# A causal convolution and a maxout layer on one core: the first tokens' chunk goes last, and the opening is put in a new order

## The chip, the cores and the metric

The kernel runs on one core of a Trainium2 chip. The metric is the device time of one execution in microseconds (us). Engines are named as in the profile: PE is TensorE (matmuls; PEld is its weight load), DVE is VectorE, ACT is ScalarE, POOL is GpSimd, and SP is the engine whose queue issues the DMAs here.

## The reference

```python
# x (8, 4160, 192), weight_gen (8, 4160, 8 heads, 7 taps); w1, w2, w3 (192, 768), w_out (768, 192)
w = np.exp(weight_gen - weight_gen.max(-1, keepdims=True))
w = w / (w.sum(-1, keepdims=True) + 1e-9)
x_pad = np.concatenate([zeros of 6 tokens, x], axis=1)
x_unf = x_pad[:, idx, :]             # for each token its own and the six tokens before it
a = np.einsum('bshk,bskhg->bshg', w, x_unf.reshape(B, S, 7, 8, 24)).reshape(B * S, 192)
h = np.maximum(np.maximum(a @ w1, a @ w2), a @ w3)
out = h @ w_out                       # (33280, 192)
```

The dense weights come as float64. The kernel sees each as a pair of 32-bit words.

## The kernel before, in words

The 33280 tokens are 260 for each of the 128 partitions. They are worked in 65 chunks of four tokens a partition (TC = 4, so 512 tokens a chunk, CH), and x and weight_gen are loaded for two chunks at a time (a "super"; the first one holds a single chunk). A super's tile of x, xt, has six tokens of halo ahead of its own. For the first tokens of a partition the halo is the tail of the partition before, or zero: such a super is loaded with a zeroing on DVE (L295, memset of the halo) and with row DMAs (L305) behind the main one (L287). There are two buffers for xt, two for wt (the softmax weights), three for the tap products r, two for the sums acc.

A chunk goes through these steps. Softmax for its super: max (DVE, L326), subtract (POOL, L331), exp (ACT, L335), sum (DVE, L340), 1e-9 added (DVE, L344), reciprocal (L348), and the product with the weights (POOL, L352). Then for each of the four tokens of a partition one product of 7 x 192 elements (POOL, L370, `r<-xt,wt`, "a tap product") and its sum over the seven taps (DVE, L382, `acc<-r`). The sums are turned so that features lie on partitions: by PE transposes (L402) for chunks 0 and 1 (ON_TENSOR = 2), by a DVE transpose and 24 block moves on ACT (L432, into `room`) for all others. The turned tokens are split into a high and a low part in the format that PE multiplies fast (xa_hi, xa_lo for features 0 to 127; xc, xb for the remaining 64).

The maxout layer uses max(a·w1, a·w2, a·w3) = a·w1 + max(0, a·(w2-w1), a·(w3-w1)). PE multiplies with the two differences (wa_hi, wa_lo, wb_hi, wb_lo; L802, `up`), ACT applies relu to the first (m, L859), DVE takes the maximum (L867), and the result is split again (h_hi on ACT, h_lo on DVE or POOL, L878). The output products (`down`, L802 too) multiply h with w_out and add a·(w1·w_out), whose matrices wca and wcb are composed once on PE (L750, 24 passes, behind turned weights, L731/L733) and split (L759, L767). The products of every group run as two halves of the PE's rows, lower and upper, at the same time; a nop on SP stands between the halves (L808), and it is queued with the DMA issues.

At the start the weights are made: each block of float64 words becomes one fp32 value by an Abs on ACT (L573), and on DVE a clamp (L579), a shift (L586) and two combinations (L595, L604). Then come differences (POOL, L631, L661) and splits (L643, L673). Blocks of 128 rows of w1, w2, w3 are called `a` (0 to 2), of the other 64 rows `b` (0 to 2), of w_out `down` or `d`.

The order of instructions on each engine is not written by hand. Each step is a `Task` with an engine, a cost, its predecessors, the buffers it holds, and a due time; `Plan.order()` plays these out with the costs and takes, on each engine, the ready task that is due first and whose buffers are free. PE's own order is fixed by the order in which its tasks are added. What comes out is the program: each engine then runs its list in that order, whatever the real durations.

Of the kernel before, what the change touches and what calls it, by code (L numbers as in the profile page):

```python
# [20 lines left out]
class Hold:  # L21


    def __init__(self, pool):
        self.pool, self.users, self.taken, self.tile = pool, 0, False, None


class Task:
    def __init__(self, engine, cost, emit, deps, due, holds, end):
        self.engine, self.cost, self.emit, self.due = engine, cost, emit, due  # L30
        self.holds, self.after = holds, []
        self.end = cost if end is None else end
        self.missing = 0
        for d in deps:
            d.after.append(self)
            self.missing += 1
        for h in holds:
            h.users += 1


class Plan:
# [4 lines left out]
    LATENCY = 0.12  # L46

    def __init__(self, pools):
        self.free = dict(pools)
        self.waiting = {"L": [], "U": []}  # L50
        self.tasks = []

    def add(self, engine, cost, emit, deps=(), due=0.0, holds=(), end=None):
# [3 lines left out]
        if engine in self.FIXED:  # L57
            self.waiting[engine].append(t)
        return t

    def order(self):
        ready, busy, events, done = {}, {}, [], []
        at = dict.fromkeys(self.FIXED, 0)
        for t in self.tasks:
            ready.setdefault(t.engine, [])
            busy.setdefault(t.engine, 0.0)
            if t.missing == 0 and t.engine not in self.FIXED:
                heapq.heappush(ready[t.engine], (t.due, t.n, t))

        def can(t):  # L70
            need = {}
            for h in t.holds:
                if not h.taken:
                    need[h.pool] = need.get(h.pool, 0) + 1
            return all(self.free[p] >= n for p, n in need.items())

        def start(t, now):
            for h in t.holds:
                if not h.taken:
                    h.taken = True  # L80
                    self.free[h.pool] -= 1
# [3 lines left out]
            heapq.heappush(events, (now + t.cost, 0, t.n, t, "free"))  # L85
            heapq.heappush(events, (now + t.end, 1, t.n, t, "given"))
            heapq.heappush(events, (now + t.end + self.LATENCY, 2, t.n, t, "seen"))

        now = 0.0
        while True:  # L90
            for e in ready:
                if busy[e] > now + 1e-9:
                    continue
                if e in self.FIXED:
                    k = at[e]
                    if k < len(self.waiting[e]):
                        t = self.waiting[e][k]
# [33 lines left out]
def lightconv_maxout_kernel(  # L131
# [29 lines left out]
    ON_TENSOR = 2  # L161
    DOWN_AT = 3
    ON_POOL = (1, 4)

# [15 lines left out]
    halves = (slice(0, DB), slice(DB, P))  # L180

# [9 lines left out]
    w1a = const.tile([P, NJ, P], F32, name="w1a")  # L191
    b32 = const.tile([P, NP, 3, P], F32, name="b32")
# [39 lines left out]
    plan = Plan(counts | {"conv": 3})  # L232
# [14 lines left out]
    def vec(n):  # L247
        return 0.15 + 0.00105 * n

    def act(n):  # L250
        return 0.18 + 0.00084 * n

    def gps(n):
        return 0.1 + 0.0024 * n


    PERIOD = 21.0
    FIRST = 22.0

    def needed(c):  # L260
        return FIRST + PERIOD * c
# [4 lines left out]
    def transfer(cost, emit, deps=(), due=0.0, holds=(), on="SP"):  # L266
        issue = plan.add(on, 0.45, emit, deps, due, holds)
        return plan.add("DMA", cost, lambda: None, [issue], due, holds, end=cost + 2.0)
# [4 lines left out]
    def load_super(s):  # L273
        cs = supers[s]
        a, n = cs[0] * TC, len(cs) * TC
        hx, hw = xts[s], wts[s] = hold("xt"), hold("wt")
        due = needed(cs[0]) - 40

# [10 lines left out]
        w = transfer(0.0005 * n * H * K, weights, (), due, [hw])  # L289
        if a >= PAD:  # L290
            t = [transfer(0.0005 * (n + PAD) * D, tokens, (), due + 0.1, [hx])]
        else:
# [4 lines left out]
            t = [transfer(0.0005 * (n + a) * D, tokens, (), due + 0.1, [hx])]  # L297
            for b in range(B):
                on = "ACT" if s == 0 and b % 2 else "SP"

                def rows(b=b, on=on):
                    to = slice(b * PB + 1, (b + 1) * PB)
                    q = nc.scalar if on == "ACT" else nc.sync
                    pin(
                        q.dma_start(  # L305
                            out=buf(hx)[to, :z], in_=xf[to.start - 1 : to.stop - 1, NT - z :]
                        )
                    )

                t.append(transfer(0.1, rows, [zero], due + 0.2, [hx], on))  # L310
# [5 lines left out]
    def softmax(s):  # L316
        n = len(supers[s]) * TC
        due = needed(supers[s][0]) - 32
# [8 lines left out]
            [loads[s][0]], due, [hr, hw],  # L327
# [4 lines left out]
            [a], due + 1, [hr, hw],  # L332
# [3 lines left out]
            [b], due + 2, [hw],  # L336
# [4 lines left out]
            [c], due + 3, [hd, hw],  # L341
        )
        e = plan.add(
            "DVE", 0.3, lambda: pin(nc.vector.tensor_scalar_add(part(hd), part(hd), 1e-9)),  # L344
            [d], due + 3, [hd],
        )
        f = plan.add(
            "DVE", 0.6, lambda: pin(nc.vector.reciprocal(part(hd), part(hd))), [e], due + 3, [hd]  # L348
# [4 lines left out]
            [f], due + 4, [hd, hw],  # L353
# [5 lines left out]
    def taps(c):  # L359
# [3 lines left out]
        due = needed(c)  # L363
        sums = []
        for t in range(TC):
            hr = hold("r")

            def product(t=t, hr=hr):
                pin(
                    nc.gpsimd.tensor_tensor(  # L370
# [661 lines left out]
```

## Time and profile before

| | us |
|---|---|
| median of 3 runs | 1440.14 (1439.23 to 1443.31) |
| profiled execution, its own time | 1444.6 |
| span in the profile | 1442.8 |
| mean granted clock of TensorE | 0.987 |
| PE busy | 1402.0 (97%) |
| ACT, POOL, DVE busy | 1117.3, 1104.2, 1043.4 |

The span is what the profile sees from the first instruction to the last; the execution's own time is 1.8 us longer. In rows of instructions the first number is the start or the busy time, as the sentence ahead says; "x36" is a count, and what follows the second bar is the idle time ahead of them with what ended it. A chunk takes 20.9 us of PE in the steady part.

### The profile page before, as it was taken

How to read it: one execution, taken by the hardware profiler on the slowest of the kernel's cores; microseconds unless marked ns; L12 is line 12 of the kernel's file. 1: busy time of each engine (PE TensorE's matmuls, PEld its weight loads, DVE VectorE, ACT ScalarE, POOL GpSimd, SP SyncE). 2: the span in 40 equal slices, each digit the busy share in tenths (PEclk: the TensorE clock that was granted, in tenths of full speed). 3: DMA queues.
4: the chain of work that ended last, by engine and by line, in shares of the span. 5: the costliest groups of instructions: out<-in, count | busy, mean ns of one | idle time of the engine just before them, and what ended most of it. 6: DMA issues, size and time to landing. Idle time of an engine off the chain costs nothing.

```text
span 1442.8 us, 37119 instructions
## 1 busy us (share of the span) xinstructions
PE 1402.0 (97%) x14878; PEld 1366.1 (95%) x14878; DVE 1043.4 (72%) x1433; ACT 1117.3 (77%) x2828; POOL 1104.2 (77%) x609
## 2 busy tenths in 40 slices
PE   2889999999999999999999999999999999999999
PEld 1579999999999999999999999999999999999998
DVE  7867777777777787777778777877877677777543
ACT  3547878878877887787788778877888887788773
POOL 6769888778877887887788778778877877787421
PEclk9679999999999999999999999999999999999999
DMA  7102111111111111111011111101111111110000
GB/s 249 46 1 79 57 68 57 68 68 57 68 46 46 57 68 68 68 57 64 28 57 68 68 68 57 68 25 67 57 68 68 57 68 44 48 57 24 23 21 26
DMA packets 23405, 85.08 MB, mean 59 GB/s; under 512 B 2768, under 2 KB 9544, under 8 KB 19136
## 3 DMA queue, kind: packets, MB, share of 16 engines
q1 hardware_dynamic: 23112, 82.44, 15.5%
q8 instruction: 116, 1.90, 0.5%
q14 instruction: 57, 0.47, 0.1%
q10 hardware_dynamic: 120, 0.28, 0.1%
HBM read 57.15 MB, written 25.56 MB: 57 GB/s over the span
## 4 chain that ended last, share of the span: by engine, by line
PE 95%; POOL 1%; DMA 1%; ACT 1%; SPq 1%; DVE 1%; issue 0%; POOLq 0%
PE bank L802 95%; POOL r L370 1%; DMA xt<-in_x_dram 1%; SPq L532 1%; DVE den L344 0%; ACT room L432 0%; DMA raw<-in_moe_w_dram 0%; SPq L516 0%; PE bank L733 0%; ACT m L859 0%; POOL wa_lo L643 0%; PE bank L731 0%; ACT wb_hi L684 0%; DVE acc L382 0%; ACT bank L573 0%
## 5 line engine op out<-in xcount | busy, mean ns | idle before, releaser
L370 POOL TENSOR_TENSOR r<-xt,wt 128x1344 f32<-128x1344 f32 x260 | 727.1, 2845 | 143.2 <-DVE acc L382 142.9
L802 PE MATMUL bank<-wo,h_hi 64*128 64x384 f32 x3120 | 675.0, 357 | 0.0
L802 PE MATMUL bank<-wo,h_lo 64*128 64x192 f32 x3120 | 603.4, 249 | 0.0
L432 ACT COPY room<-room 32x128 f32<-32x128 f32 x1512 | 448.4, 297 | 79.0 <-DVE room L421 55.9
L802 PEld LDWEIGHTS bank<-wo,h_lo 64*128 64x128 f32 x3120 | 493.0, 188 | 0.0
L802 PEld LDWEIGHTS bank<-wo,h_hi 64*128 64x128 f32 x3120 | 489.2, 186 | 0.0
L802 PE MATMUL bank<-xa_hi,wa_hi 64*128 64x512 f32 x1560 | 479.9, 394 | 6.0 <-ACT wa_hi L637 3.4
L802 PE MATMUL bank<-xa_hi,wa_lo 64*128 64x512 f32 x1560 | 477.9, 390 | 3.4 <-POOL wa_lo L643 3.3
L802 PE MATMUL bank<-xa_lo,wa_hi 64*128 64x512 f32 x1560 | 476.8, 391 | 0.5 <-DVE xa_lo L460 0.5
L382 DVE TENSOR_REDUCE acc<-r 128x192 f32<-128x1344 f32 x260 | 399.8, 1538 | 0.6 <-POOL r L370 0.3
L859 ACT ACTIVATE m<-bank 128x512 f32<-128x512 f32 x390 | 234.5, 601 | 71.4 <-PE bank L802 66.7
L935 DVE TENSOR_TENSOR o<-bank,ob 128x192 f32<-128x192 f32 x260 | 92.4, 356 | 268.7 <-ACT ob L928 268.5
L802 PE MATMUL bank<-xb,wb_hi 64*128 64x512 f32 x780 | 284.5, 390 | 0.3 <-DVE xb L465 0.3
L802 PE MATMUL bank<-xc,wb_hi 64*128 64x512 f32 x780 | 281.1, 390 | 0.2 <-ACT wb_hi L684 0.2
L802 PEld LDWEIGHTS bank<-xa_hi,wa_hi 64*128 64x128 f32 x1560 | 255.3, 186 | 13.5 <-ACT wa_hi L637 4.3
L802 PEld LDWEIGHTS bank<-xa_hi,wa_lo 64*128 64x128 f32 x1560 | 255.3, 186 | 11.2 <-POOL wa_lo L643 5.6
L802 PEld LDWEIGHTS bank<-xa_lo,wa_hi 64*128 64x128 f32 x1560 | 254.9, 187 | 6.4 <-DVE xa_lo L460 1.5
L802 PE MATMUL bank<-xc,wb_lo 64*128 64x512 f32 x780 | 258.0, 389 | 0.0
L867 DVE TENSOR_TENSOR bank<-bank,m 128x512 f32<-128x512 f32 x260 | 179.0, 689 | 42.2 <-PE bank L802 24.3
L878 POOL TENSOR_TENSOR h_lo<-m,h_hi 128x512 fp32r<-128x512 f32 x130 | 171.7, 1321 | 40.0 <-ACT h_hi L871 39.9
L802 PE MATMUL bank<-wca,xa_hi 64*128 64x384 f32 x520 | 183.4, 353 | 0.0
L878 DVE TENSOR_TENSOR h_lo<-bank,h_hi 128x512 fp32r<-128x512 f32 x260 | 172.4, 681 | 11.4 <-ACT h_hi L871 11.2
(79 smaller groups left out, 2012.5 us busy)
## 6 DMA issues: line engine op xcount, KB each, us to landing
xt<-in_x_dram SPq DMA_DIRECT2D x31, 1344.0 KB, 5.8
out_dram<-o SPq DMA_DIRECT2D x64, 384.0 KB, 2.3
wt<-in_weight_gen_dram SPq DMA_DIRECT2D x32, 224.0 KB, 2.6
h_hi<-in_moe_w_dram SPq DMA_DIRECT2D x6, 256.0 KB, 2.9
xt<-in_x_dram SPq DMA_DIRECT2D x1, 1152.0 KB, 5.8
h_lo<-in_moe_w_dram SPq DMA_DIRECT2D x6, 128.0 KB, 4.0
raw<-in_moe_w_dram SPq DMA_DIRECT2D x3, 256.0 KB, 3.6
room<-in_moe_w_out_dram SPq DMA_DIRECT2D x2, 384.0 KB, 6.4
```

Source lines behind the costliest of these rows:

```text
L370: nc.gpsimd.tensor_tensor(buf(hr).rearrange("p (h g) k -> p k h g", g=G), buf(hx)[:, la + t : la + t + K].rearrange("p k (h g) -> p k h g" ...
L382: pin(nc.vector.tensor_reduce(buf(ha)[:, t], buf(hr), axis=AX.X, op=ALU.add))
L432: pin(nc.scalar.copy(to[:, :, p : p + 32], b[p : p + 32, :, f : f + 32]))
L532: nc.sync.dma_start(out=raw_b()[h, jps[0] : jps[-1] + 1, i].rearrange("p j n w -> p j (n w)"), in_=w[P:].rearrange("p (j o n) -> p j o n", ...
L802: ins = nc.tensor.matmul(buf(hb)[:, :n], w()[h], v()[h], start=half == 0 and first, stop=half == 1 and last,)
L859: lambda: pin(nc.scalar.activation(buf(hm), buf(hb), AF.Relu)), [made], due,
L867: lambda: pin(nc.vector.tensor_tensor(buf(keep), buf(hb), buf(hm), op=ALU.max)),
L878: eng.tensor_tensor(buf(hl)[:, j], buf(keep), buf(hh)[:, j].bitcast(F32), op=ALU.subtract)
L935: nc.vector.tensor_tensor(buf(ho)[:, t], buf(hb)[:, :D], buf(hq), op=ALU.add)
```

## The change

Five things are changed.

1. `place` maps the chunk that the program works on to the tokens that it holds: the program's chunks 0, 1, 2 ... 62 are the tokens' chunks 2, 3 ... 64, and its last two are the tokens' chunks 0 and 1. So the super with the halo rows is the last one. Its row DMAs become four with strided partitions (64, 32, 16 and 8 rows).
2. The due times are no longer worked out from a period: `start_by` goes backwards from the tasks that have one. Costs are new (DVE 0.062 + 0.00104 n instead of 0.15 + 0.00105 n, ACT's block moves 0.31 instead of 0.296, a tap product 2.68 instead of 2.75), the latency is 0.1, and at most eight DMAs are counted in flight.
3. The order in which the opening's tasks are added is written out (`OPENING`), with times for its loads (`LOAD_DUE`).
4. Engines in the opening: three of the first eight tap products go to DVE; eight clamps go to POOL (through a tile `m`, since POOL doesn't get the bank); the differences of a block's two matrices are made together where they can be; the difference of the last `b` block goes to PE (`minus`); two splits go to DVE (L762); POOL takes h_lo of three of six blocks in chunks 0 and 1 rather than two. The `b` loads are six DMAs, not twelve.
5. The 1e-9 is added on ACT (L395), in each super.

```diff
+    place = [*range(2, NC), 0, 1]
-        a, n = cs[0] * TC, len(cs) * TC
+        a, n = place[cs[0]] * TC, len(cs) * TC
...
+            step = 2
+            while step <= PB:
+                def rows(step=step):
+                    to = buf(hx)[step // 2 :: step, :z]
+                    of = xf[step // 2 - 1 :: step, NT - z :][: P // step]
+                    pin(nc.sync.dma_start(out=to, in_=of))
...
+    def start_by(self):
+        for t in reversed(self.tasks):
+            latest = [a.by - self.LATENCY - t.end for a in t.after]
+            if t.due is not None:
+                latest.append(t.due)
+            t.by = min(latest, default=1e6)
...
+    ON_POOL_FIRST = (0, 1, 5)
+    TAPS_ON_VECTOR = ((0, 3), (1, 0), (1, 2))
+    CLAMP_ON_POOL = (("a", 1, 0), ("a", 1, 1), ("a", 2, 0), ("a", 2, 1), ("a", 2, 2), ("b", 1), ("d", 0), ("d", 1),)
...
         e = plan.add(
-            "DVE", 0.3, lambda: pin(nc.vector.tensor_scalar_add(part(hd), part(hd), 1e-9)),
+            "ACT", 0.25,
+            lambda: pin(nc.scalar.activation(part(hd), part(hd), AF.Copy, bias=1e-9)),
...
+            eng, cost = ("DVE", vec(D * K)) if (c, t) in TAPS_ON_VECTOR else ("POOL", 2.68)
...
-                got.append(plan.add("ACT", 0.296, move, [turned], due - 11 + q, [hv]))
+                got.append(plan.add("ACT", 0.31, move, [turned], clock[0] - 2 + q, [hv]))
```

The zeroing of the last super's halo still has no predecessor, and holds its xt buffer from then on.

The new line numbers that matter: clamp L659, shift L665, combinations L674 and L683, tap product L428, sum L440, differences L731, split of the weights L762, products L922, maximum L987, h_lo L998, x loads L337 (L339 and L357 for the last super), weight_gen L332.

DVE in the opening, from the point where the first chunk's sums begin. The kernel before:

```order
L326 TENSOR_REDUCE red<-wt 128x64
L382 TENSOR_REDUCE acc<-r 128x192
L579 TENSOR_SCALAR bank<-bank 128x384
L604 SCALAR_TENSOR_TENSOR wx<-h_hi,bank 128x256
L382 TENSOR_REDUCE acc<-r 128x192
L586 TENSOR_SCALAR bank<-bank 128x384
L595 SCALAR_TENSOR_TENSOR bank<-h_hi,bank 128x256
L382 TENSOR_REDUCE acc<-r 128x192
```

And the changed one, at the same point:

```order
L376 TENSOR_REDUCE red<-wt 128x64
L428 TENSOR_TENSOR r<-xt,wt 128x7x192
L440 TENSOR_REDUCE acc<-r 128x192 x2
L659 TENSOR_SCALAR bank<-bank 128x384 x2
L665 TENSOR_SCALAR bank<-bank 128x384 x2
L674 SCALAR_TENSOR_TENSOR bank<-h_lo,bank 128x384 x2
L683 SCALAR_TENSOR_TENSOR b_68<-h_lo,bank 128x384 x2
L440 TENSOR_REDUCE acc<-r 128x192 x2
```

Sixteen rows stand ahead of the first sum before and 26 now; a tap product on DVE is new, and the sums stand two and two.

SP's queue, from its first row, with the tiles' numbers (xt_135 and so on are uses, not addresses). The kernel before:

```order
L280 DMA wt_133<-in_weight_gen_dram 128x224
L287 DMA xt_135<-in_x_dram 128x768
L516 DMA h_hi_138<-in_moe_w1_dram 128x512
L305 DMA xt_135<-in_x_dram 15x1152 x4
L516 DMA h_hi_138<-in_moe_w2_dram 128x512
L516 DMA h_hi_138<-in_moe_w3_dram 128x512
```

The changed one, behind a first block of the same three weight loads:

```order
L598 DMA h_hi_134<-in_moe_w1_dram 128x512
L598 DMA h_hi_134<-in_moe_w2_dram 128x512
L598 DMA h_hi_134<-in_moe_w3_dram 128x512
L332 DMA wt_144<-in_weight_gen_dram 128x224
L337 DMA xt_146<-in_x_dram 128x1920
L332 DMA wt_150<-in_weight_gen_dram 128x448
```

And nine rows further on, from the last super's load:

```order
L339 DMA xt_136<-in_x_dram 128x1536
L357 DMA xt_136<-in_x_dram 64x1152
L357 DMA xt_136<-in_x_dram 32x1152
L357 DMA xt_136<-in_x_dram 16x1152
L357 DMA xt_136<-in_x_dram 8x1152
L337 DMA xt_262<-in_x_dram 128x2688
L332 DMA wt_277<-in_weight_gen_dram 128x448
L337 DMA xt_668<-in_x_dram 128x2688
```

Two blocks of the weights now head the queue. xt_136 is the last super's x: it is loaded in the opening and read by POOL's last tap products, at the program's end. It holds one of the two xt buffers till then.

POOL in the steady part, around the last tap product of one super and the first of the next, with the tiles' numbers. The kernel before:

```order
L370 TENSOR_TENSOR r_8454<-xt_7231,wt_7222 128x7x192
L460 TENSOR_TENSOR xa_lo_8532<-room_8215,xa_hi_8516 128x512
L465 TENSOR_TENSOR xb_8553<-room_8215,xc_8528 64x512
L370 TENSOR_TENSOR r_8620<-xt_7231,wt_7222 128x7x192
L878 TENSOR_TENSOR h_lo_8366<-m_8598,h_hi_8334 128x512
L370 TENSOR_TENSOR r_8687<-xt_7952,wt_7943 128x7x192
```

The changed one, at the same point:

```order
L428 TENSOR_TENSOR r_8639<-xt_7973,wt_7250 128x7x192
L998 TENSOR_TENSOR h_lo_8703<-m_8685,h_hi_8674 128x512
L549 TENSOR_TENSOR xb_8861<-room_8570,xc_8819 64x512
L544 TENSOR_TENSOR xa_lo_8880<-room_8570,xa_hi_8856 128x512
L403 TENSOR_TENSOR wt_7983<-wt_7983,den_8816 128x448
L381 TENSOR_TENSOR wt_8692<-wt_8692,red_8858 128x448
L428 TENSOR_TENSOR r_8931<-xt_8682,wt_7983 128x7x192
```

One step stands between the two products before, five now.

More of the change, by code (lines that the diff above doesn't have):

```diff
@@ L296, in load_super @@
             )
[L297 to L310, printed above, removed]
+            t = [transfer(0.38 * (n + a), tokens, (), due + 0.1, [hx])]
+            step = 2
[4 more added lines that the diff above has]
+                    pin(nc.sync.dma_start(out=to, in_=of))
+                t.append(transfer(0.38 * z / step, rows, [zero], due + 0.2, [hx]))
+                step *= 2
         loads[s] = w, t
@@ new lines, in difference, with rest, differences_a @@
+        return lambda: buf(hb)[:, : n * m].rearrange("p (i n) -> p i n", i=n), d, [hb]
+    def rest(size, to, of, hi, deps, holds, on):
+        eng = nc.gpsimd if on == "POOL" else nc.vector
+        return plan.add(
+            on, gps(size) if on == "POOL" else vec(size),
+            lambda: pin(eng.tensor_tensor(to(), of(), hi(), op=ALU.subtract)), deps, None, holds,
+        )
+    def differences_a(jp, first, last):
+        pair = slice(2 * jp, 2 * jp + 2)
+        hx, got = of_bank["x", jp]
+        on, then = MODE["a", jp]
+        n = last - first
+        v, d, holds = difference(
+            (n, 2 * P), lambda: buf(hx)[:, first:last],
+            lambda: w1a[:, pair].rearrange("p j n -> p (j n)"), [*got[first:last], one_a[jp]],
+            [hx], on,
+        )
+        of = lambda: v().rearrange("p i (j n) -> p i j n", j=2)
+        place_of = lambda w: w[:, pair, first:last].rearrange("p j i n -> p i j n")
+        hi = plan.add(
+            "ACT", act(2 * n * P), lambda: pin(nc.scalar.copy(place_of(wa_hi), of())), [d], None,
+            holds,
+        )
+        lo = rest(
+            2 * n * P, lambda: place_of(wa_lo), of, lambda: place_of(wa_hi).bitcast(F32), [hi],
+            holds, then,
+        )
+        for i in range(first, last):
+            w_hi[jp, i], w_lo[jp, i] = hi, lo
@@ L939, in down @@
         )
-        a = c * TC
+        a = place[c] * TC
         if c == NC - 1:
@@ L951, in down @@
             )
-    made = plan.add("POOL", 1.0, lambda: make_identity(nc, ident), (), -50)
-    for s in range(len(supers)):
-        load_super(s)
-    load_a(0)
-    load_b([0])
-    load_a(1)
-    load_b([1, 2])
-    load_a(2)
-    load_down()
-    for s in range(len(supers)):
-        softmax(s)
-    for jp in range(NP):
-        prepare_a(jp)
-        prepare_b(jp)
-    for q in range(NP):
-        prepare_down(q)
-    def tokens(c):
-        parts(c, *blocks(c, *taps(c), u_last() + [made]))
@@ L992, in lightconv_maxout_kernel, with downs, ups, singles_down @@
-    for c in (NC - 2, NC - 1):
+    made = plan.add("POOL", 1.0, lambda: make_identity(nc, ident), (), -60)
+    made_minus = plan.add(
+        "ACT", 0.25, lambda: pin(nc.scalar.activation(minus, ident, AF.Copy, scale=-1.0)),
+        [made], -40,
+    )
+    def tokens(c):
+        parts(c, *blocks(c, *taps(c)))
+    def downs(c):
         for t in range(TC):
             down(c, t)
+    def ups(c, j):
+        for i in range(NI):
+            up(c, j, i)
+    def singles_down():
+        for q in range(NP):
+            prepare_down(q)
@@ new lines, in lightconv_maxout_kernel @@
+    step = {
+        "load": load_super, "load a": load_a, "load b": load_b, "load down": load_down,
+        "softmax": softmax, "singles": singles, "singles down": singles_down, "taps": opening_taps,
+        "turn x": turn_tokens, "parts": opening_parts,
+        "a": differences_a, "b": differences_b, "up": ups,
+        "turn": turn_weights, "compose": compose, "down": downs,
+    }
+    for what, *which in OPENING:
+        step[what](*which)
+    for c in range(2, NC):
+        s = super_of[c]
+        if s > 1 and supers[s][0] == c:
+            load_super(s)
+            softmax(s)
+        if c >= ON_TENSOR:
+            tokens(c)
+        for j in range(DOWN_AT):
+            ups(c, j)
+        if c < NC - 1:
+            downs(c - 1)
+        for j in range(DOWN_AT, NJ):
+            ups(c, j)
```

399 lines of the change are left out of this document (218 added, 181 removed), and 6 rows, old and new, of the table OPENING.

## The prediction

> **What bounds the kernel now.** I read the page first, for what ends last.
>
> ```profile
> PE 1402.0 (97%) x14878; PEld 1366.1 (95%) x14878; DVE 1043.4 (72%) x1433; ACT 1117.3 (77%) x2828; POOL 1104.2 (77%) x609
> PE 95%; POOL 1%; DMA 1%; ACT 1%; SPq 1%; DVE 1%; issue 0%; POOLq 0%
> ```
>
> PE is 97% busy, and it is 95% of the chain that ended last. The end of that chain says from when on:
>
> ```profile
> 87.88 4.04 DVE den L344
> 91.92 0.26 DVE wcb L767
> 92.22 1347.23 PE bank L802 x12536
> ```
>
> From 92.22 us PE works without a gap for 1347.23 us. So a change can win in three ways only: PE reaches the same point of its work sooner, PE runs at a better clock after it, or PE has less to do. It can lose if another engine's cycle grows past PE's. PE's waits, first those in the first 92.2 us, then those after 92:
>
> ```profile
> PE bank L402 <- DVE acc L382: 21.8, 4, 16.6
> PE bank L802 <- DVE wcb L767: 5.2, 1, 5.2
> ```
>
> In the opening PE waits for the sums of the tap products; its last wait, 5.2 us, ends at 92.2. Stretches of time (columns: window, its length, busy us and counts of PE, PEld, DVE, ACT, POOL, PE clock, DMA share, GB/s):
>
> ```profile
> 0.00:92.22 92.22, 54.81 (x223) 39.11 (x223) 69.03 (x114) 41.76 (x100) 69.49 (x54) 0.85 0.35 115
> 40.00:50.00 10.00, 8.95 (x39) 6.27 (x38) 6.21 (x13) 7.56 (x19) 8.94 (x8) 0.67 0.00 1
> 91.00:101.00 10.00, 8.78 (x50) 8.78 (x51) 4.49 (x5) 0.00 (x0) 6.09 (x3) 0.51 0.00 0
> 101.00:111.00 10.00, 10.00 (x115) 9.96 (x114) 7.18 (x9) 3.63 (x8) 3.90 (x3) 0.98 0.08 30
> 400.90:442.70 41.80, 41.80 (x460) 41.07 (x458) 31.27 (x43) 34.29 (x88) 33.76 (x19) 1.00 0.16 59
> ```
>
> In the opening no engine is full: DVE and POOL have 69 of 92.2 us, and the clock is at 0.67 between 40 and 50. After the last wait it stands at 0.51, and PE gets 50 matmuls done in ten microseconds where it does 115 in the next ten. The last row is one steady super (two chunks): PE 41.80 of 41.80 us, POOL next with 33.76.
>
> **PE's own work up to the point of 92.2 us.** Rows: the first and the last of six groups in the opening (36, 36, 36, 18, 18 and 18 half-array matmuls, 162 together), a warm pair and a cold pair, and ten of the 24 compose passes.
>
> ```profile
> L802 PE MATMUL bank<-xa_hi,wa_lo 64*128 64x512 f32 x36 | 18.0, 544 | 3.4 <-POOL wa_lo L643 3.3
> L802 PE MATMUL bank<-xc,wb_lo 64*128 64x512 f32 x18 | 8.9, 507 | 0.0
> 109.28 0.39 PE L802 MATMUL bank<-xa_hi,wa_lo 64*128 64x512 f32 x1
> 109.51 0.39 PE L802 MATMUL bank<-xc,wb_lo 64*128 64x512 f32 x1
> 36.36 0.62 PE L802 MATMUL bank<-xa_hi,wa_lo 64*128 64x512 f32 x1
> 36.79 0.62 PE L802 MATMUL bank<-xa_hi,wa_hi 64*128 64x512 f32 x1
> 84.75 1.79 PE L750 MATMUL bank<-wo,raw 128*128 128x192 f32 x10
> ```
>
> The 162 make 81 pairs, both halves at once. A pair starts every 0.23 us warm (109.28 to 109.51) and every 0.43 cold (36.36 to 36.79). So chunk 0's 54 pairs and the first 27 of chunk 1 are 18.6 us warm, and 24 passes at 0.179 are 4.3. The rest of the 92.2 us is waiting and cold clock; the changed kernel has the same pairs and the same passes ahead of chunk 0's output products.
>
> **The new opening, by DVE.** The changed order puts conversions, sums and one tap product in one dense row on DVE. Prices:
>
> ```profile
> h_hi<-in_moe_w_dram SPq DMA_DIRECT2D x6, 256.0 KB, 2.9
> 0.74 0.39 SPq L280 DMA_DIRECT2D wt<-in_weight_gen_dram  x1
> 10.77 0.43 DVE L586 TENSOR_SCALAR bank<-bank 128x256 uint32<-128x256 uint32 x1
> 11.11 0.42 DVE L579 TENSOR_SCALAR bank<-bank 128x256 f32<-128x256 f32 x1
> 11.44 0.42 DVE L595 SCALAR_TENSOR_TENSOR bank<-h_hi,bank 128x256 uint32<-128x256 uint32 x1
> L586 DVE TENSOR_SCALAR bank<-bank 128x384 uint32<-128x384 uint32 x6 | 3.3, 556 | 0.0
> L382 DVE TENSOR_REDUCE acc<-r 128x192 f32<-128x1344 f32 x14 | 21.6, 1545 | 0.3 <-POOL r L370 0.3
> L370 POOL TENSOR_TENSOR r<-xt,wt 128x1344 f32<-128x1344 f32 x17 | 44.9, 2708 | 0.3
> ```
>
> SP's first issue stands at 0.74; that slot now belongs to a 256 KB weight block, which lands after 2.9, at 3.6. With the first Abs on ScalarE (0.4, like DVE's pass of that width) DVE starts at 4.0. Passes of 256 follow each other every 0.33 us (10.77, 11.11, 11.44: 0.42 with 0.09 overlapped); with the same overlap one of 384 costs 0.47 and a sum 1.46. Ahead of PE's first products, whose place in PE's order is behind the last weight turn, DVE has 25 passes of 256 (8.3), eleven of 384 (5.2), four sums (5.8), one tap product and the softmax's small steps (1.4, by their 224 and 448 elements). The eight clamps that POOL takes are not among them; on DVE they would be 3.1 more over the opening. A tap product on DVE is not in the trace: from below DVE's sum over as many elements, 1.46; from above POOL's 2.71; I take 1.46, the same engine's row. Together 22.2: DVE alone is there at 26.2. It also waits for POOL, which has three of the four products at 2.71 behind the softmax's steps; I put that at 4.0, between nothing and the 8.1 of three products in a row: 30.2. With the turns and ScalarE's copy behind it, 1.2, PE's first product stands at 31.4. Before, it stood a little ahead of the cold pair at 36.4.
>
> From 30.2 to compose, which needs every conversion of w_out, DVE's row holds seven passes of 256 (2.3), ten of 384 (4.7), ten steps over 512 (0.6 each by the same slope, 6.0: five maxima, two h_lo, xa_lo, xb, wa_lo), two small reductions and a reciprocal (1.5), two taps (2.9) and four sums (5.8). That is 23.2, done at 53.4, and at 56.4 with 3.0 more for POOL. PE's 54 pairs fill 12.4 warm, or 23.2 if all were cold, of the 25.0 since its first product, so they don't bind. Compose is 4.3 warm, twice that cold; PE stands idle ahead of it, so I take the middle, 6.5: 62.9. Then 27 pairs at 0.23, 6.2, and 1.9 for parts of chunk 1 that come late: X = 71.0, against 92.2. That is 21.2 won.
>
> **The cold stretch.** The window from 91 shows 50 matmuls where 115 fit: 9.2 us at half speed cost 4.6. In the changed kernel PE is dense from compose on, so I count 4.6, with nothing as the other end.
>
> **The steady part and the x buffers.** The last super's zeroing has nothing to wait for, so one of the two x buffers is taken at the start and used at the end; 31 supers share the other. An x load then waits for POOL's last tap of the super before.
>
> ```profile
> xt<-in_x_dram SPq DMA_DIRECT2D x31, 1344.0 KB, 5.8
> 437.12 2.86 POOL L370 TENSOR_TENSOR r<-xt,wt 128x1344 f32<-128x1344 f32 x1
> 439.76 1.04 POOL L331 TENSOR_TENSOR wt<-wt,red 128x448 f32<-128x448 f32 x1
> 441.13 1.29 POOL L465 TENSOR_TENSOR xb<-room,xc 64x512 fp32r<-64x512 f32 x1 [0.33 <-PE bank L802]
> 442.50 1.30 POOL L460 TENSOR_TENSOR xa_lo<-room,xa_hi 128x512 fp32r<-128x512 f32 x1
> 444.72 0.98 POOL L352 TENSOR_TENSOR wt<-wt,den 128x448 f32<-128x448 f32 x1 [0.92 <-DVE den L348]
> POOL r L370 <- DVE acc L382: 142.9, 57, 3.2
> SPq L280 <- POOL r L370: 14.7, 28, 0.9
> POOL xa_lo L460 <- ACT xa_hi L444: 62.5, 30, 7.6
> ```
>
> The load takes 5.8 us and an issue 0.4. The plan lays five other POOL steps into it: the four rows behind the product (L331, L465, L460, L352) are 4.6, and an h_lo, as wide as L460, 1.3: 5.9. POOL's cycle is 33.8 busy, 0.3 uncovered, and 142.9/32 = 4.5 of waits on DVE: 38.6, under 41.8. So nothing is lost where these steps are ready; where none is, 33.8 + 6.2 + 4.5 = 44.5, 2.7 a super. SP queues the nops between PE's halves behind that load, so SP's waits of up to 0.9 become PE's as soon as POOL is late. I take 2 us in all, near the covered end, for the first supers.
>
> **Edits that cost nothing.** The twelve 64-row loads become six of twice the size and the 16 row loads four strided ones, off SP's opening queue's head and, for x, at the end's buffer, 1300 us ahead of use. The block moves' price (0.296 to 0.31) only changes the order; ScalarE has 34.3 of 41.8. POOL taking three h_lo of chunks 0 and 1 lies beside PE's pairs; if POOL is late there, chunk 1's sums are. The minus matmuls on PE are three cold passes ahead of T0, beside DVE. The 1e-9 step goes from DVE to ScalarE:
>
> ```profile
> L344 DVE TENSOR_SCALAR den<-den x33: 181/1186/4124, 7.4 to 1278.4; 128x64 f32<-128x64 f32 x32, 128x32 f32<-128x32 f32 x1
> 87.79 4.12 DVE L344 TENSOR_SCALAR den<-den 128x64 f32<-128x64 f32 x1
> 84.07 7.80 POOL L370 TENSOR_TENSOR r<-xt,wt 128x1344 f32<-128x1344 f32 x3
> ```
>
> It takes 0.18 at best, 1.19 in the middle, and once 4.12: that one ended at 91.91 with POOL's three products at 91.87. So some DVE steps on SBUF wait until a run of POOL is over, and the 4.04 of it in the chain goes with the move. The four new DVE steps with two SBUF inputs (three taps, one wa_lo) may wait likewise: by the median row 1.0 each, 4.0; the sum holds 7.0 of waits for these and for POOL's lateness together; by the longest, 3.9 each, 15.6. The Trainium skill, "SBUF — State Buffer", § Who interferes with whom, has a rule for it that speaks against the change: a DVE instruction with two SBUF inputs contends with a GpSimd instruction that reads SBUF, and the other fully blocks; by it the sum would go to the 15.6 end where POOL never pauses, by the row's median it holds the 4.0. The trace agrees that a block lasts to the end of POOL's run; whether a two-input step is blocked no row here shows.
>
> **Sum.** 21.2 + 4.6 - 2.0 = 23.8 off the profiled execution, 1444.6 (span 1442.8 and 1.8 around it), which stands 4.5 over the median of 1440.14. Against the median I forecast 1440 - 22 = 1418, giving back 1.8 for waits that I may have missed.
>
> **Rivals.**
> (a) One x buffer costs a little in each super, 0.2 to 0.6 of the 2.7 above: 31 x 0.2 to 0.6 is 6 to 19, 1424 to 1437. For it: POOL's waits on DVE come 57 times, up to 3.2. Against: 3.2 us of slack per super.
> (b) Slower: none of the five steps is ready when the load runs. POOL's cycle of 44.5 goes over 41.8, 2.7 x 31 = 84, 1500. It decides where more than 3.5 of the load's 6.2 is uncovered (41.8 - 33.8 - 4.5), and beyond 4.3 the opening's gain is gone (23.8 / 31 = 0.8). For it: POOL's xa_lo has waited for ScalarE 30 times, up to 7.6, and such waits would now add to the load. Against: POOL is idle for 8.0 of the steady super's 41.8, and they are in these already.
> (c) DVE's taps wait for POOL's long runs: up to 15.6 instead of 4.0 in DVE's row, 6 to 11.6 less won, 1424 to 1430.
> (d) The clock falls again after compose's wait: 4.6 not won, 1422. The Trainium skill, "TensorE: Matmul & The Clock Gate", § Part 1, says that the clock rises after one busy window of some 3.4 us and falls after an idle one; the 0.51 after the wait of 5.2 agrees. With no wait of that length left, the sum stays at 1418.
> (e) DVE waits for POOL not at all: 7.0 more, 1411.
> (f) The opening is only reordered and PE's work still meets the last weight conversion at 92: then 1440 within 4. Against: no engine is full in the opening.
>
> **Chances.** Forecast with its spread of 5 (1413 to 1423, with (d)) 0.56, (e) 0.12, (c) 0.13, (a) 0.11, (b) 0.05, (f) 0.03. The range 1409 to 1429 takes in (c) and (e) and leaves out (b), (f) and most of (a). 0.3% is 4.3 us, about what a measurement here can tell: faster 0.91, same 0.03, slower 0.06.
>
> **What would show it.** PE's last wait should end at 65 to 76, DVE be over 90% busy from 4 to 55, and the clock read 0.9 or more in the ten microseconds after that wait. Right on the buffer: x loads wait for L428 on POOL, POOL for the x load under 1 us each. Wrong: waits of PE on SP or on POOL's r past 100 us (b), or L428 on DVE at 3 us and more (c).

## The result, and the profile after

| | before | after |
|---|---|---|
| median, us | 1443.31 (1440.14 in the first three runs) | 1434.17 (1433.03 to 1434.33) |
| ratio | | 0.9946 (95% interval 0.9929 to 0.9963) |
| span of the profiled execution | 1442.8 | 1432.4 |
| first output product of chunk 1 starts | 117.28 | 96.56 |
| first output product of chunk 61 starts | 1371.25 | 1360.87 |

One of the five executions of the kernel before took 7508.24 us; it counts in the median of 1443.31 (without it the middle is 1441.7), and it is left out of the ratio.

The forecast was 1418 (1409 to 1429): right in direction, wrong in size. The last two lines of the table say where. At chunk 1 the changed kernel is 20.7 us ahead; 60 chunks later it is 10.4 ahead, and so it ends. The opening won 20.7 of the 25.8 us that it was to win, and the steady part gave half of that back, 10.3 us. These are the four rows, first those of the kernel before, then of the changed one:

```profile
117.28 0.33 PE L802 MATMUL bank<-wca,xa_hi 64*128 64x384 f32 x1
1371.25 0.33 PE L802 MATMUL bank<-wca,xa_hi 64*128 64x384 f32 x1
```

```profile
96.56 0.33 PE L922 MATMUL bank<-wca,xa_hi 64*128 64x384 f32 x1
1360.87 0.33 PE L922 MATMUL bank<-wca,xa_hi 64*128 64x384 f32 x1
```

Below, "pace" is the time from chunk 5's first output product to chunk 61's, divided by 56: 20.89 us a chunk before, 21.07 after.

**The opening.** PE's waits of the changed kernel, and windows of its opening (columns as in the prediction):

```profile
PE bank L853 <- DVE b L683: 17.2, 1, 17.2
PE bank L851 <- DVE w1a L683: 7.3, 2, 6.3
PE bank L481 <- DVE acc L440: 2.7, 2, 1.5
PE bank L481 <- DVE h_lo L998: 0.8, 1, 0.8
PE bank L922 <- ACT wb_hi L805: 0.3, 1, 0.3
```

```profile
50.00:60.00 10.00, 7.13 (x23) 4.72 (x24) 10.00 (x15) 2.59 (x5) 9.82 (x5) 0.52 0.00 0
60.00:70.00 10.00, 10.00 (x36) 8.65 (x35) 6.33 (x10) 4.58 (x10) 8.08 (x5) 0.63 0.00 0
75.50:85.50 10.00, 10.00 (x128) 9.96 (x127) 5.11 (x8) 8.93 (x29) 8.48 (x5) 1.00 0.28 114
```

PE's last wait of the opening ends at 54.9, where it ended at 92.2 before, and DVE is full from 50 to 60. The cold stretch has moved: it lies at 50 to 67 and covers the last pairs of chunk 0 and most of the compose passes; behind the first output products (75.55) the clock is at 1.00.

**The steady part hides its loss.** After 75 us the list of PE's waits is empty, and PE counts as busy all the time:

```profile
200.00:1300.00 1100.00, 1099.03 (x11903) 1057.34 (x11900) 797.59 (x1073) 893.96 (x2299) 892.47 (x475) 1.00 0.16 58
```

The same window of the kernel before:

```profile
200.00:1300.00 1100.00, 1100.00 (x12024) 1085.35 (x12022) 821.42 (x1108) 902.07 (x2294) 889.39 (x476) 1.00 0.16 58
```

The busy time is nearly equal; the count is not. 11903 matmuls where 12024 went through is 1.0% less, at a full clock. A wait this short hardly shows as idle time of PE, since the last matmuls ahead of it are drawn to a modelled end, here 499.69. The starts within one half show it, here ahead of the last h_lo of a chunk:

```profile
499.04 0.36 PE L922 MATMUL bank<-wo,h_hi 64*128 64x384 f32 x1
499.24 0.25 PE L922 MATMUL bank<-wo,h_lo 64*128 64x192 f32 x1
499.33 0.36 PE L922 MATMUL bank<-wo,h_hi 64*128 64x384 f32 x1
499.74 0.35 PE L922 MATMUL bank<-wo,h_lo 64*128 64x192 f32 x1
```

From h_hi's product to h_lo's it is 0.41 us, where the pair ahead of it took 0.20 (499.04 to 499.24). There is such a gap at 415.58, 499.74 and 583.87, always at the first token's last h_lo, once in four chunks. It need not be hunted for: the weight loads (PEld) have a list of waits of their own, and that one isn't empty. The row of the weight load behind the gap, and the list from 180 to 1355 us:

```profile
499.74 0.18 PEld L922 LDWEIGHTS bank<-wo,h_lo 64*128 64x128 f32 x1 [0.31 <-DVE h_lo L998]
PEld bank L922 <- DVE h_lo L998: 6.2, 24, 0.4
PEld bank L922 <- POOL xb L549: 1.9, 7, 0.5
PEld bank L922 <- POOL xa_lo L544: 0.4, 1, 0.4
```

In the kernel before this list is empty over the same stretch. So 6.2 us of waits for h_lo (24, half of them at these gaps and half, of 0.2, two chunks behind each) and 2.3 for POOL's xb and xa_lo make up 8.5 of the 10 us that the pace loses; waits of 0.11 us, which the trace has once in four chunks too, are not in the list. The chain of waits goes back from there along DVE; its timeline:

```profile
491.37 0.98 DVE L506 STREAM_TRANSPOSE room<-acc 128x768 f32<-128x768 f32 x1 [0.24 <-POOL xb L549]
492.27 0.65 DVE L998 TENSOR_TENSOR h_lo<-bank,h_hi 128x512 fp32r<-128x512 f32 x1
492.85 0.67 DVE L987 TENSOR_TENSOR m<-bank,m 128x512 f32<-128x512 f32 x1
493.44 2.99 DVE L440 TENSOR_REDUCE acc<-r 128x192 f32<-128x1344 f32 x2
496.35 1.29 DVE L987 TENSOR_TENSOR bank<-bank,m 128x512 f32<-128x512 f32 x2
497.55 1.54 DVE L440 TENSOR_REDUCE acc<-r 128x192 f32<-128x1344 f32 x1
499.01 1.28 DVE L998 TENSOR_TENSOR h_lo<-bank,h_hi 128x512 fp32r<-128x512 f32 x2
```

From the turning at 491.37 to the h_lo at 499.01 DVE runs without a pause. Three sums of tap products, 4.4 us, stand in its order ahead of the h_lo that PE needs; a later chunk's sums are served first.

### The profile page after: what moved, and what is told of

Read it like the earlier page. It is cut to its first block, busy times and chain, and to the rows that moved or that the text cites. A ratio compares the mean times of both kernels' runs of the same rounds, so it can differ in the third digit from the quotient of the medians.

```text
span 1432.4 us, 37054 instructions
## 1 busy us (share of the span) xinstructions
PE 1399.5 (98%) x14884; PEld 1341.8 (94%) x14884; DVE 1021.9 (71%) x1394; ACT 1117.7 (78%) x2860; POOL 1105.1 (77%) x609
## 4 chain that ended last, share of the span: by engine, by line
PE 77%; POOL 9%; DVE 8%; issue 3%; ACT 2%; DMA 0%; SPq 0%; DVEq 0%; POOLq 0%
PE bank L922 76%; POOL r L428 6%; DVE acc L440 3%; DVE bank L987 2%; DVE h_lo L998 1%; POOL h_lo L998 1%; POOL xb L549 1%; POOL xa_lo L544 1%; ACT h_hi L991 1%; DVE m L987 1%; ACT room L517 1%; ACT m L979 0%; POOL wt L403 0%; PE bank L870 0%; DVE r L428 0%
## 5 line engine op out<-in xcount | busy, mean ns | idle before, releaser
L428 POOL TENSOR_TENSOR r<-xt,wt 128x1344 f32<-128x1344 f32 x257 | 715.4, 2853 | 22.3 <-DMA xt<-in_x_dram 19.0
L922 PE MATMUL bank<-wo,h_hi 64*128 64x384 f32 x3120 | 660.1, 355 | 0.0
L922 PE MATMUL bank<-wo,h_lo 64*128 64x192 f32 x3120 | 593.5, 249 | 0.9
L922 PE MATMUL bank<-xa_hi,wa_hi 64*128 64x512 f32 x1560 | 507.9, 392 | 0.4 <-ACT wb_hi L805 0.3
L922 PE MATMUL bank<-xa_lo,wa_hi 64*128 64x512 f32 x1560 | 507.2, 391 | 0.0
L922 PE MATMUL bank<-xa_hi,wa_lo 64*128 64x512 f32 x1560 | 502.8, 388 | 0.0
L922 PEld LDWEIGHTS bank<-wo,h_lo 64*128 64x128 f32 x3120 | 482.5, 187 | 8.0 <-DVE h_lo L998 6.2
L922 PEld LDWEIGHTS bank<-wo,h_hi 64*128 64x128 f32 x3120 | 475.3, 185 | 0.0
L440 DVE TENSOR_REDUCE acc<-r 128x192 f32<-128x1344 f32 x260 | 398.2, 1543 | 18.9 <-POOL r L428 18.5
L998 POOL TENSOR_TENSOR h_lo<-m,h_hi 128x512 fp32r<-128x512 f32 x132 | 174.2, 1320 | 179.9 <-ACT h_hi L991 179.7
L922 PE MATMUL bank<-xc,wb_hi 64*128 64x512 f32 x780 | 295.7, 388 | 0.0
L922 PE MATMUL bank<-xb,wb_hi 64*128 64x512 f32 x780 | 280.4, 390 | 0.1
L922 PE MATMUL bank<-xc,wb_lo 64*128 64x512 f32 x780 | 276.5, 388 | 0.0
L922 PEld LDWEIGHTS bank<-xa_lo,wa_hi 64*128 64x128 f32 x1560 | 266.9, 185 | 9.2 <-POOL xa_lo L544 0.4
L922 PEld LDWEIGHTS bank<-xa_hi,wa_hi 64*128 64x128 f32 x1560 | 264.7, 185 | 10.5 <-ACT raw L858 0.8
L922 PEld LDWEIGHTS bank<-xa_hi,wa_lo 64*128 64x128 f32 x1560 | 265.1, 185 | 8.5
L987 DVE TENSOR_TENSOR bank<-bank,m 128x512 f32<-128x512 f32 x258 | 175.6, 694 | 81.7 <-PE bank L922 62.0
L998 DVE TENSOR_TENSOR h_lo<-bank,h_hi 128x512 fp32r<-128x512 f32 x258 | 172.5, 680 | 51.2 <-ACT h_hi L991 49.9
L991 ACT CAST h_hi<-bank 128x512 fp32r<-128x512 f32 x258 | 151.1, 586 | 66.6 <-DVE bank L987 63.3
```

The source lines that it names most:

```text
L428: on.tensor_tensor(to, buf(hx)[:, la + t : la + t + K].rearrange("p k (h g) -> p k h g", g=G), buf(hw)[:, la + t] .rearrange("p (h k) -> p ...
L440: pin(nc.vector.tensor_reduce(buf(ha)[:, t], buf(hr), axis=AX.X, op=ALU.add))
L922: ins = nc.tensor.matmul(buf(hb)[:, :n], w()[h], v()[h], start=half == 0 and first, stop=half == 1 and last,)
L987: lambda: pin(nc.vector.tensor_tensor(buf(keep), buf(hb), buf(hm), op=ALU.max)),
L991: "ACT", act(CH), lambda: pin(nc.scalar.copy(buf(hh)[:, j], buf(keep))), [m], due + 1,
L998: eng.tensor_tensor(buf(hl)[:, j], buf(keep), buf(hh)[:, j].bitcast(F32), op=ALU.subtract)
```

## The experiments

Theory A was the one that I had at hand: the single x buffer (rival a). Theory C came from the rows above: the order on DVE. Three kernels ran first on A, with one on the opening. The cuts of code below are shortened. The kernel before, run again beside the experiments in three sittings, had medians of 1442.75, 1443.24 and 1441.84, so a difference of some 1.5 us between two rows from different sittings says nothing.

**Two x buffers in the changed kernel** (e1).

```diff
-  zero = plan.add("DVE", 1.1, memset, (), due, [hx])
+  zero = plan.add("DVE", 1.1, memset, [ready[s - 2]] if s > 2 else (), due, [hx])
```

> The changed kernel, but the zeroing of the last super's halo has a predecessor (the softmax weights of the super two before it), so that both x buffers serve all supers. Theory A, one x buffer costs the steady part 0.18 us a chunk (pace 21.07 us where it was 20.89): the pace goes back to 20.89 and the time to 1434 - 10 = 1424. Theory B, the plan's new costs or the 1e-9 on ScalarE cost it: the pace stays at 21.05 to 21.10 and the time at 1433 to 1435.

Measured: 1451.4 (1449.63 to 1453.83), pace 21.23. Slower than with one buffer; theory A fails here, and theory B's 1433 to 1435 isn't what came either. The profiled execution is 15.5 us over the changed kernel's: its first output product is 2.5 earlier, 9.1 are lost in the stretch from chunk 1's to chunk 2's output products (30.05 instead of 20.98, the opening's order differs too), and 8.7 in the pace. It has the same gap, wider (910.18 to 911.02), once a super.

**The place of the chunks alone, in the kernel before** (e2): `place` as in the change, nothing else.

> The kernel before, with the place of the chunks alone changed (its own opening order, costs and engines; the halo rows load in sixteen parts as before, now at the end). Its last super's zeroing takes an x buffer from the start too. Theory A: the pace worsens from 20.89 by 0.1 to 0.25 us a chunk, 6 to 15 us in all, and the opening gains 0 to 6 from the halo rows' loads: 1440 to 1455. Theory B: the pace stays within 0.03 of 20.89, and the time is 1434 to 1441.

Measured: 1480.22, pace 21.45, slower than either theory's range. Here the single buffer does cost, though the order changed with it. POOL's waits, which have no such line before:

```profile
POOL r L371 <- DMA xt<-in_x_dram: 129.4, 28, 9.0
```

They reach PE: its weight loads wait 16.2 us for POOL's xa_lo, in 26 waits. In the changed kernel the line above reads 19.0 us over 13 waits. So one buffer costs what an order leaves uncovered of the load: up to 9.0 us at a time with the old order, little with the new one.

**The place undone in the changed kernel** (e3).

```diff
-    place = [*range(2, NC), 0, 1]
+    place = [*range(NC)]
```

> The changed kernel with the chunks in their natural places: the halo rows and the zeroing are in the opening again, both x buffers serve from there on. Theory A: pace 20.89, and the opening later by 0 to 5 us for the halo loads: 1424 to 1429. Theory B: pace 21.05 to 21.10, 1434 to 1439. That the place itself is what wins the opening: the first products start 5 us later or more than at 33.

Measured: 1449.07, pace 21.24, first output product at 79.29. With two buffers in e1 it starts at 73.02, so the halo loads in the opening cost some 6 us (the orders differ a little elsewhere too). The pace is e1's, though the place is the old one: again not the buffer. Neither theory's time came. The first product of PE stands at 37.50, 4.5 us later than the changed kernel's 32.95, and in e1, which keeps the new place, at 36.59; so these runs don't show that the place brings the first products forward. Even without the place the output products start at 79.29, so most of what the opening won comes from its new order, engines and costs, which no run takes apart further.

**No tap products on DVE** (e5).

```diff
-    TAPS_ON_VECTOR = ((0, 3), (1, 0), (1, 2))
+    TAPS_ON_VECTOR = ()
```

> The changed kernel with all tap products on POOL. If DVE and POOL hold each other up (three taps took 9.1 us of DVE where the sum of that size takes 1.5, and three of POOL's took 9.9 beside one of them where 8.1 would do): POOL's four first products end at 25 as now, DVE has 9 us less from 14 to 60, and the output products of the first chunk start 2 to 5 us earlier than at 75.6: 1429 to 1432. If the taps on DVE do win time, POOL's three more products (8 us) make the opening 3 to 8 us later: 1437 to 1442. The pace stays at 21.07 in both.

Measured: 1432.42, pace 20.89. The first output product is at 70.53, 5.0 us earlier, and compose starts at 57.74 rather than 62.74. But then chunks 1 and 2 take 23.2 and 32.9 us, the chain of waits there going through the block moves of their tokens, and 14 us are lost. I had not seen that coming, nor the pace: an edit of the opening alone moved the pace of all that follows back to 20.89. That suggests an order that the planner settles into.

**The sum and the last h_lo change places** (e6), in the finished order and there alone (the condition is put in words):

```diff
+    order = plan.order()
+    for lo in last_h_los:            # of each chunk
+        if row_ahead_on_DVE(lo) is a sum, and neither its buffer nor acc is taken up in between:
+            move that sum behind lo
-    for t in plan.order():
+    for t in order:
```

> The changed kernel with one local edit of the finished order: wherever a sum of tap products (L440) stands on DVE directly ahead of a chunk's last h_lo, the two change places; 55 places, all else stays. Theory C, the steady part is slow because DVE's order puts the sums of the tap products ahead of the last h_lo that PE's output products wait for (gaps of 0.45 at 415.6, 499.7 and 583.9): the pace goes from 21.07 to 20.87 to 20.95 and the time from 1434 to 1424 to 1428. Theory D, DVE has too much to do in those ten microseconds whatever the order, and POOL then waits for the product's buffer instead: the pace stays at 21.02 to 21.10, the time at 1431 to 1436.

Measured: 1429.08 (1428.52 to 1430.43), pace 20.98, between the ranges of C and D. The weight loads' waits from 180 to 1355 us:

```profile
PEld bank L928 <- POOL xb L555: 4.2, 12, 1.0
PEld bank L928 <- POOL xa_lo L550: 1.2, 1, 1.2
```

The waits for h_lo are all gone with one row moved, and just over half of the loss with them. What is left are waits for POOL's xb and xa_lo, longer than the 2.3 us of the changed kernel, and most of them early: from chunk 13 to chunk 61 the pace is 20.91, where the changed kernel has 21.05 and the kernel before 20.89. There the swap wins back more than four fifths of the loss.

**The same with two x buffers** (e7).

> The same local edit on the kernel with two x buffers (57 places), which has a pace of 21.23 and gaps of 0.83 at the same matmul, once a super. Theory C: the pace falls to 20.87 to 21.0 and the time from 1451 to 1433 to 1440. Theory D: the pace stays above 21.15, 1447 to 1453.

Measured: 1435.99, pace 20.93 against 21.23: 15 us faster than e1. From chunk 13 on the pace is 20.90 against 21.25. Theory D falls here and C's ranges hold; in e6 C's mechanism holds, though its ranges were missed, the time by 1 us and the pace by 0.03.

**The 1e-9 on DVE again** (e4).

```diff
-            "ACT", 0.25, activation(part(hd), part(hd), AF.Copy, bias=1e-9)
+            "DVE", 0.3, tensor_scalar_add(part(hd), part(hd), 1e-9)
```

> The changed kernel with the 1e-9 added on DVE again. Theory E, the step on ScalarE lengthens the softmax's chain and so makes POOL's weights late: the pace returns to 20.9, 1424. Theory C: only the order changes a little; wherever the pace is above 20.95, PE's gaps are at a chunk's last h_lo; without that, no more than 33 x 1.0 us of DVE time that nothing waits for, 1431 to 1437.

Measured: 1424.51, pace 20.89. That is theory E's number, and C's 1431 to 1437 was missed; but C had let the order change, so it is not refuted by this. Two kernels separate the engine from the order: the changed order with the step on DVE (e9), and e4's order with the step on ScalarE (e10).

```diff
# e9: planned as ("ACT", 0.25), run as tensor_scalar_add on DVE
# e10: planned as ("DVE", 0.3), run as an activation on ScalarE
```

> The changed kernel with the 1e-9 on DVE, but put where the changed order has it: planned as a step of ScalarE, so the other rows of every engine keep their order; DVE runs it at that place. Theory E (the step's engine costs the pace): 20.9 and 1424, as where it was planned on DVE. Theory C (the order costs it): no better than 21.05, 1433 or more; on top of that the step may wait for a run of POOL's products, 1 to 4 us a super in front of the sums, which in this order could reach PE: up to 1510.

> The reverse: the order that comes out with the 1e-9 planned on DVE (pace 20.89, 1424.5), with the step then run on ScalarE at that place. Theory E: the pace goes back to 21.05 to 21.1, 1434. Theory C: it stays at 20.87 to 20.92, 1422 to 1427.

Measured: e10 1423.62 (1423.35 to 1423.97), pace 20.88; e9 1473.83 (1458.57 to 1477.59), pace 21.52 in its profile. Theory E falls. e10 has the changed kernel's engines and its one x buffer, and is 10.5 us faster by the order alone; its weight loads have no wait from 180 to 1355 us. Its DVE timeline at the same place of a chunk (output products from 535.96):

```profile
528.79 0.98 DVE L505 STREAM_TRANSPOSE room<-acc 128x768 f32<-128x768 f32 x1 [1.05 <-POOL xb L548]
529.70 0.67 DVE L986 TENSOR_TENSOR bank<-bank,m 128x512 f32<-128x512 f32 x1
531.22 0.69 DVE L986 TENSOR_TENSOR m<-bank,m 128x512 f32<-128x512 f32 x1 [0.85 <-PE bank L921]
531.82 0.68 DVE L997 TENSOR_TENSOR h_lo<-bank,h_hi 128x512 fp32r<-128x512 f32 x1
532.42 1.54 DVE L439 TENSOR_REDUCE acc<-r 128x192 f32<-128x1344 f32 x1
533.88 0.69 DVE L986 TENSOR_TENSOR bank<-bank,m 128x512 f32<-128x512 f32 x1
534.48 1.54 DVE L439 TENSOR_REDUCE acc<-r 128x192 f32<-128x1344 f32 x1
535.94 0.68 DVE L997 TENSOR_TENSOR h_lo<-bank,h_hi 128x512 fp32r<-128x512 f32 x1
```

The turning comes 7.2 us ahead of the output products, not 6.1, and two sums stand between, not three. The last h_lo is done at 536.6; PE takes it at 537.75. So it is there 1.1 us before PE needs it, where the changed kernel's holds PE up.

e9 shows what the step can meet on DVE. Its row, and then POOL's rows at that time:

```profile
1003.95 8.04 DVE L395 TENSOR_SCALAR den<-den 128x64 f32<-128x64 f32 x1
```

```profile
1001.53 5.47 POOL L428 TENSOR_TENSOR r<-xt,wt 128x1344 f32<-128x1344 f32 x2
1006.86 1.30 POOL L544 TENSOR_TENSOR xa_lo<-room,xa_hi 128x512 fp32r<-128x512 f32 x1
1008.12 1.27 POOL L549 TENSOR_TENSOR xb<-room,xc 64x512 fp32r<-64x512 f32 x1
1009.36 2.58 POOL L428 TENSOR_TENSOR r<-xt,wt 128x1344 f32<-128x1344 f32 x1
```

The DVE step ended at 1011.99, POOL's run at 1011.94. It was held up over five POOL instructions. With such waits in it e9 shows only that the engine doesn't bring the pace back in the changed order; it is e10 that isolates the order.

**The block moves' price undone** (e8): 0.31 back to 0.296.

> The changed kernel with the planner's price of a block move at 0.296 instead of 0.31 (nothing else on the chip differs but the order). Theory F, the price keeps the plan nearer the chip (rows show 0.296 busy and 0.31 from start to start), so undoing it costs 2 to 8 us: 1436 to 1442. Theory C: the price only picks another order; the pace may come out anywhere from 20.87 to 21.25, and where it is above 20.95 PE's gaps are at the last h_lo. The opening, up to the output products of the first chunk, is the same within 0.5 us.

Measured: 1435.27, pace 21.09, first output product at 75.47 (75.55). The ranges of the two kernels overlap (1434.04 to 1435.62 against 1433.03 to 1434.33), so I count 1 us at most; theory F's 2 to 8 us are not there.

**The planner's old costs** (e11).

> The changed kernel with the planner's old costs (DVE 0.15 + 0.00105 n, ACT 0.18 + 0.00084 n, POOL 0.1 + 0.0024 n, sum 1.55, tap product 2.75, turning 0.97, block move 0.296, latency 0.12). Theory G, costs above the chip's durations leave slack in the order and so keep PE's pace: 20.87 to 20.92, and with an opening of 76 to 85 the time is 1424 to 1433. Theory C: old or new, the costs pick an order whose pace is whatever its burst on DVE makes it: 20.9 to 21.25; the opening is later by 3 to 12 us, 1430 to 1450.

Measured: 1433.34 (1430.75 to 1433.86), pace 20.99, first output product at 77.01. Its pace lies between what G and the changed kernel give, and its opening is 1.5 us later, not the 3 to 12 of C: neither theory forecast all of this. Its waits are in neither of PE's two lists, so where its 0.1 us a chunk goes is open. The new costs, as a whole, gain nothing that this measurement can tell from the old.

**The clamps back on DVE** (e12): `CLAMP_ON_POOL = ()`.

> The changed kernel with all clamps on DVE. If DVE's row binds the opening, eight clamps more are 3.1 us: the output products of the first chunk start at 77 to 80 instead of 75.6. If POOL binds it, they start at 73 to 76. The order behind the opening changes too, so the time may be anything from 1428 to 1445; PE's start of the first output products and the pace are what is read.

Measured: 1442.25, first output product at 73.55, pace 21.08. The eight clamps on POOL did not make that point earlier; it is 2.0 us later with them. Without them it is 30.4 us from chunk 1's to chunk 2's output products, where the changed kernel takes 21.0, and that is where the time goes. The 3.1 us that I had put on DVE for them don't show at this point.

In one table, from the profiles (the medians are of the runs):

| kernel | first output product | pace | median |
|---|---|---|---|
| before (first two at 86.5, the rest after its last wait) | 92.2 | 20.89 | 1443.31 |
| changed | 75.6 | 21.07 | 1434.17 |
| e1 two x buffers | 73.0 | 21.23 | 1451.40 |
| e6 h_lo ahead | 74.6 | 20.98 | 1429.08 |
| e7 two x buffers, h_lo ahead | 78.1 | 20.93 | 1435.99 |
| e4 1e-9 on DVE | 76.8 | 20.89 | 1424.51 |
| e10 e4's order, 1e-9 on ScalarE | 76.2 | 20.88 | 1423.62 |

The last two beat both kernels: e10 has a ratio to the kernel before of 0.9873 (0.9857 to 0.9890).

## Why the prediction was wrong, point by point

**What the miss adds up to.** The forecast was 16.2 us too low: the opening won 5.1 less than forecast and the steady part lost 8.3 more, and 2.7 came from taking 22 off the median of 1440.14 where the sum of 23.8 belonged to an execution of 1444.6.

**DVE's start and row: right, then short.** Its first conversion started at 3.92 (forecast 4.0), and PE's first product at 32.95 (31.4). What the prediction says of the kernel before, that this product stood a little ahead of 36.4, is a misreading: it stood at 26.33, with waits of PE behind it. So the changed kernel starts its products 6.6 us later and works them in a denser row. DVE's conversions for compose were done at 60.2 (56.4). What was mis-sized is the two-input steps:

```profile
14.13 2.56 DVE L428 TENSOR_TENSOR r<-xt,wt 128x1344 f32<-128x1344 f32 x1 [1.17 <-POOL wt L403]
37.52 2.91 DVE L762 TENSOR_TENSOR wa_lo<-wx,wa_hi 128x512 fp32r<-128x512 f32 x1
41.14 6.39 DVE L428 TENSOR_TENSOR r<-xt,wt 128x1344 f32<-128x1344 f32 x2
```

```profile
14.17 9.91 POOL L428 TENSOR_TENSOR r<-xt,wt 128x1344 f32<-128x1344 f32 x3
41.96 2.98 POOL L998 TENSOR_TENSOR h_lo<-m,h_hi 128x512 fp32r<-128x512 f32 x1 [1.95 <-ACT h_hi L991]
44.89 3.33 POOL L381 TENSOR_TENSOR wt<-wt,red 128x448 f32<-128x448 f32 x1
```

I took 1.46 for a tap product on DVE, 0.6 for wa_lo; they took 2.56, 3.2 and 3.2, and 2.91. That is 6.9 us over, as much as the 7.0 that the sum had set aside for all waits on POOL; the plain waits came on top. And POOL pays too, which the sum left out: three products 9.91 instead of 8.1, h_lo 2.98 for 1.3, the softmax's step 3.33 for 0.98. The rule of the Trainium skill, "SBUF — State Buffer", § Who interferes with whom, that a DVE instruction with two SBUF inputs contends with one of GpSimd that reads SBUF, agrees with these rows. How much of a row is the step's own price and how much a wait is not settled: wa_lo began inside a POOL product (37.32 to 40.01) and ended 0.4 us behind it, but the first tap product began at 14.13, ahead of POOL's at 14.17, and the pair at 41.14, while POOL stood idle until 41.96. So 1.46 may be too low for a tap product even alone. The prediction's sign for rival (c), a tap product on DVE of 3 us and more, did come, with 3.2 twice; no one step showed the 3.9 more of its far end. In e5, without the three taps, the first output product came 5.0 us earlier.

**"54 pairs don't bind": wrong.** PE's order puts chunk 1's token turns between chunk 0's last pairs, and these waited for DVE (the 2.7 and 0.8 above). The clock fell, and the pairs behind ran cold: compose began at 62.74, 2.5 us after DVE was done. Compose itself took 6.39 (forecast 6.5), and from there to the output products it was 6.4, not 8.1. X, where the output products begin, is 75.55, not 71.0.

**The cold stretch: right in size.** 16.7 us at the output products became 20.7 at chunk 1: 4.0 for 4.6. The opening as a whole won 20.7 of the 25.8. The signs named for it failed all the same: PE's last wait was to end at 65 to 76 and ended at 54.9, and the clock behind it was to read 0.9 and read 0.50 in the next ten microseconds. DVE was to be over 90% busy from 4 to 55 and was: 47.6 of 51.0 us.

**"I take 2 us in all" for the steady part: the step that failed most.** It was 10.3. Rival (a) had 6 to 19 us and a chance of 0.11, and its time of 1424 to 1437 is what came; but its mechanism did not. The x loads were mostly covered: POOL waited 19.0 us for them in all, 0.6 a super, though in 13 waits of 1.0 to 2.8 us, where the prediction's sign was under 1 us each. What PE waited for was h_lo, 6.2 of its weight loads' 8.5 us of waits. The step asked only whether POOL's cycle fits under PE's. POOL's cycle did fit; what it did not ask is whether each result that PE waits for is made in time within the chunk. A mean of 31.3 busy of 41.8 us on DVE says nothing on the eight microseconds ahead of one h_lo.

**The edits at no cost.** The step to ScalarE changed nothing by its engine (e10 against e4), and the moves' price next to nothing (e8). (The `b` loads are 192 KB each, for 128 and 64 before, not twice the size; nothing rests on it.) But each edit that enters the planner picks another order, and that had a price of 10 us here, which no part of the sum looked for.

What is shown: the waits at the last h_lo, that moving one row removes them and recovers 5 us, and that another order of the same work recovers 10.5. The other half of the loss in e6 (its pace is 20.98, e10's 20.88) is waits for POOL's xb and xa_lo, most of them ahead of chunk 13. Not settled is why the planner lands in either order.

## What to carry to other kernels

Where a planner sets the order, every change to its inputs is also a change of the order: compare the pace of the steady part in both traces before crediting the edit, and separate the two by running the old step in the new order and the reverse. On a bounding engine that is "100% busy" with an empty list of waits, read the list of its weight loads too, count instructions over a long window and look at the starts within one half of its rows; e11 shows that even both lists can miss a wait. And what matters on a half-idle engine is what stands directly ahead of the result that the bounding engine needs next.

## What the runs showed of the hardware that I had not expected

- A DVE step on SBUF of 0.19 us took up to 8.04 beside POOL (e9, 33 such steps). Four of them took 8.0 us, over five POOL instructions, and ended with POOL's run. Eight took 4.2 to 4.5, over three, and ended 0.05 us after the third (xa_lo), while POOL went on without a pause. So such a wait lasts over several instructions of POOL here, but not always until its run is over, as the prediction had it from one row; what lets the step in is open.
- DVE and POOL side by side may be no faster than one after the other: from 41.14 DVE's two tap products took until 47.53, and POOL's h_lo and softmax step, 2.3 us elsewhere, until 48.22. At the 1.46 that I estimated for a product on DVE alone, which no run shows, the four would be 5.2 in a row; at the 2.56 of the first product they would be 7.4, against the 7.1 that they took.
- The clock of the changed kernel fell at about 50.4, with PE never idle for more than 1.5 us at a time. Ahead of it one half of the rows had run dry: PE counts as busy, with half the matmuls.

```profile
46.00:47.00 1.00, 1.00 (x13) 0.96 (x10) 1.00 (x1) 0.00 (x0) 1.00 (x1) 1.00 0.00 0
48.00:49.00 1.00, 1.00 (x6) 0.82 (x5) 1.00 (x2) 0.85 (x2) 0.22 (x1) 1.00 0.00 0
49.00:50.00 1.00, 0.42 (x2) 0.00 (x0) 1.00 (x2) 0.70 (x2) 0.37 (x1) 1.00 0.03 8
51.00:52.00 1.00, 0.00 (x0) 0.00 (x0) 1.00 (x1) 0.88 (x2) 1.00 (x1) 0.50 0.00 0
```

From 13 matmuls a microsecond it goes to 6, then 2; the clock is at 0.50 from 51 on, and full again at 68. The Trainium skill, "TensorE: Matmul & The Clock Gate", § Part 1, speaks of an idle window of some 3.4 us ahead of the fall; here the 3.4 us ahead of it held 2.4 with one half at work and 0.8 idle.
